# Kernel generation with integer turns and bit-wise fractions, and statistics of eight token tiles moved to ScalarE

## The chip, the cores and the metric

The kernel runs on one core of a Trainium2 chip. The metric is the device time of one execution in microseconds (us), as the median over runs. The engines named below are TensorE (PE; PEld are its weight loads), VectorE (DVE), ScalarE (ACT), GpSimd (POOL) and SyncE (SP, which here only issues transfers). They run side by side; each works through its own instructions in order and waits on semaphores for the others.

## The reference

Four residual layers over x of 2048 tokens and 640 channels: a long convolution (a), attention (b), the same convolution (c), the same attention (d).

```python
def _A_ref(u, A_re, A_im, B_re, B_im, C_re, C_im, log_dt, Dskip):
    dt = jnp.exp(log_dt)[:, None]
    logdA = dt * (A_re + 1j * A_im)
    dB = dt * (B_re + 1j * B_im)
    P = jnp.exp(logdA[:, :, None] * l[None, None, :])        # l = 0..2047
    K = jnp.einsum("dn,dnl,dn->dl", Cc, P, dB).real          # 640 channels, 128 states
    ...                                                      # causal convolution of u with K by FFT
    return y + u * Dskip

x = A_u
x = x + _A_ref(_layernorm(x), ...)
x = x + _B_ref(_layernorm(x), ...)                           # 32 heads, one shared key/value head
x = x + _A_ref(_layernorm(x), ...)
x = x + _B_ref(_layernorm(x), ...)
```

## The kernel before, in words

**Generation of the convolution kernels (`_kgen`, L360).** K[d, l] is a sum over 128 complex exponentials. The position l is split as 32 i + col, so that exp(logdA l) is a product of two factors, each with a size (a real exponential) and an angle. The 640 channels are worked in 20 units of 32 channels. For every unit and each of two halves h (h = 0 the factor over i, h = 1 the factor over col and the phase of C times B):

- `phase_first` (L416): TensorE makes the angles, in turns, as [128, 1024] in PSUM, tile `ph`, which has one buffer.
- `phase` (L424): VectorE takes the whole turns away. `magic_round` (L240, the instruction has L241) adds and subtracts 1.5 * 2^23 into `r` (bf16), then L431 subtracts `r` from `ph` into `f`, a fraction between -1/2 and 1/2; `f` has four buffers.
- `trig` (L433): ScalarE makes `fa` = |f| (L444), sin(2 pi f) (L445) and cos as sin(pi/2 - 2 pi |f|) (L446).
- `sizes` (L449) and `exps` (L457): TensorE makes the exponents in PSUM (`pe`, two buffers, three tiles a unit), ScalarE the exponentials (L462, L464).
- `products` (L466): six VectorE instructions of 128x1024 multiply sizes and sines. `sums` (L483): TensorE sums over the 128 states into `pk`. `store` (L494): ScalarE copies `pk` out, and transfers take it to memory.

The order on TensorE, ScalarE and VectorE is written out by hand in the loop from L519 on: in turn u it works on unit u with `trig`, `sizes` and `exps`, on unit u + 1 with `phase`, on unit u - 1 with `products`, on unit u - 2 with `sums` and on unit u - 3 with `store`. Sine and exponential need different tables on ScalarE; even and odd units therefore order them differently, and one pair of units loads each table once. In turns 5 to 12 VectorE also takes the layer norm's statistics of token tiles 0 to 7 (`stats`, L680: two `bn_stats`, one `bn_aggr`); tiles 8 to 15 follow behind the last unit. In the last turns the weights of the Fourier transform (`wf`, 4 MB) are loaded into the memory that the tables of the generation leave (L578).

**Spectra of the kernels (`kernel_spectra`, L781).** For five chunks of 128 channels, `raw` (L616) makes four products on TensorE, which ScalarE copies out (L631), and `whole` (L645) is a set of butterflies on VectorE (L642, L118, L121) through the common buffer `B`. `raw` of a chunk stands ahead of `whole` of the chunk before it in the order, and takes a hook `ahead(t)` that is called ahead of each of its four products. The spectra are stored to memory and loaded again in the convolution.

**Normalization.** `norm` (L754) turns the statistics `mv` into scale and shift for two groups of token tiles: eight small VectorE instructions and one square root on ScalarE (L747) for each. In `conv_layer` (L802) both calls stand ahead of `kernel_spectra`. The scaled input is first needed by `prepare(0)` (L894, L830) behind the spectra.

The convolution, the attention and layers c and d are not touched.

Of the kernel before, what the change touches and what calls it, by code (L numbers as in the profile page):

```python
# [11 lines left out]
F32 = mybir.dt.float32  # L12
F32R = mybir.dt.float32r
BF16 = mybir.dt.bfloat16
I32 = mybir.dt.int32
AF = mybir.ActivationFunctionType
ALU = mybir.AluOpType
# [4 lines left out]
P = 128  # L22
L = 2048
D = 640
# [4 lines left out]
TWO_PI = 2.0 * math.pi  # L29
# [4 lines left out]
FIRST = (0, 2, 1, 3)  # L34
TAUS = [s + 4 * n for s in FIRST for n in range(4)]
SCALE = 20.0**-0.5
LIMIT = 32.0 * 20.0**0.5
SAFE = ((LIMIT - 1e-6) / 1.002) ** 2
LOG2 = SCALE / math.log(2.0) * 2.0**23
LOWEST = -125.0 * math.log(2.0) / SCALE  # L40
# [149 lines left out]
def weave(calls, between):  # L190

    for i in range(len(calls) + 1):
        for n, call in between:
            if n == i or (i == len(calls) and n > i):
                call()
        if i < len(calls):
            calls[i]()


class Net:  # L200
# [8 lines left out]
    def setup(self, ctx):  # L209
        tc, nc = self.tc, self.nc  # L210
        self.cp = ctx.enter_context(tc.tile_pool(name="cp", bufs=1))
        self.dr = ctx.enter_context(tc.tile_pool(name="dr", bufs=1, space=DRAM))
        self.ident = self.cp.tile([P, P], F32, name="ident")
        self.halfpi = self.cp.tile([P, 1], F32, name="halfpi")
        nc.vector.memset(self.halfpi, 0.5 * math.pi)
        self.xp = ctx.enter_context(tc.tile_pool(name="xp", bufs=1))
        self.x = self.xp.tile([P, 16, D], F32, name="x")
        self.mv = [self.xp.tile([P, 12, 2], F32, name="mv0"), self.xp.tile([P, 4, 2], F32, name="mv1")]
        self.rn = None
        self.placed = {}  # L220
        self.kd = self.dr.tile([NCH, P, 16 * DC], F32, name="kd")
        self.kh = self.dr.tile([NCH, P, 32 * DC], F32, name="kh")
# [137 lines left out]
    def _kgen(self, ctx):  # L360
        tc, nc, ins = self.tc, self.nc, self.ins
        kp = ctx.enter_context(tc.tile_pool(name="kps", bufs=1, space=PSUM))
        early = ctx.enter_context(ExitStack())
# [31 lines left out]
        bp = ctx.enter_context(tc.tile_pool(name="kgb", bufs=2, reuse_waits="tile"))  # L395
# [1 line left out]

        units = [(q, r, q * 256 + 16 * r, 128, 128) for q in range(2) for r in range(8)]
        units += [(2, r, 512 + 16 * r, 64, 64) for r in range(4)]
        C1, S1, C2, S2, M1, M2, E1R, F, PH, PE_, PK, KST = ({} for _ in range(12))  # L400
        KST[0, 0] = bp.tile([P, 64, 32], F32, tag="kst", bufs=2, name="kst00")

        def big(tag, u, x, bufs=2):
# [17 lines left out]
                nc.tensor.matmul(pp[:, 512 * par : 512 * par + 512], grp(src, u, par, rows),  # L421
                                 kg[0:rows, col : col + 512], start=True, stop=True)

        def phase(u, h):  # L424
            if (u, h) not in PH:
                phase_first(u, h)
            pp = PH.pop((u, h))
            r = bp.tile([P, 1024], BF16, tag="r", bufs=2, name=f"r{u}{h}")
            self.magic_round(r, pp)
            F[u, h] = bp.tile([P, 1024], F32, tag="f", bufs=4, name=f"f{u}{h}")  # L430
            nc.vector.tensor_tensor(F[u, h], pp, r, ALU.subtract)  # L431

        def trig(u, h):  # L433
            if h == 0:
                C1[u], S1[u] = big("c1", u, 33), big("s1", u, 33)
                nc.gpsimd.memset(C1[u][:, :, :, 0:1], 1.0)
                nc.gpsimd.memset(S1[u][:, :, :, 0:1], 0.0)
                s, c = swap(S1[u])[:, :, :, 1:33], swap(C1[u])[:, :, :, 1:33]
            else:
                C2[u], S2[u] = big("c2", u, 32, 3), big("s2", u, 32, 3)  # L440
                s, c = swap(S2[u]), swap(C2[u])
            f = F.pop((u, h))
            fa = bp.tile([P, 1024], F32, tag="fa", bufs=1, name=f"fa{u}{h}")
            nc.scalar.activation(fa, f, AF.Abs)  # L444
            nc.scalar.activation(s, f.rearrange("p (a d s) -> p a d s", a=2, d=16), AF.Sin, scale=TWO_PI)  # L445
            nc.scalar.activation(c, fa.rearrange("p (a d s) -> p a d s", a=2, d=16), AF.Sin,  # L446
                                 scale=-TWO_PI, bias=self.halfpi)

# [65 lines left out]
        n = len(units)  # L514
        engines = {mybir.EngineType.PE, mybir.EngineType.Activation, mybir.EngineType.DVE}
        with tc.manual_schedule(engines=engines):
            for h in range(2):
                phase(0, h)
            for u in range(n + 3):  # L519
                now, nxt, prod, tot = u < n, u + 1 < n, 0 < u <= n, 2 <= u < n + 2  # L520
                odd = u % 2 == 1
                if u >= 3:
                    store(u - 3)
                if now and not odd:
                    trig(u, 0)
                if prod:
                    products(u - 1, 0)
                if now:
                    sizes(u, 0)
                    if odd:  # L530
                        exps(u, 0)
                if nxt:
                    phase_first(u + 1, 0)
                if tot:
                    sums(u - 2, range(0, 2))
                if now:
                    sizes(u, 1)
                    if odd:
                        exps(u, 1)
                if tot:  # L540
                    sums(u - 2, range(2, 3))
                if nxt:
                    phase(u + 1, 0)
                if now and odd:
                    sizes(u, 2)
                    exps(u, 2)
                if prod:
                    products(u - 1, 1)
                if now:
                    trig(u, 0 if odd else 1)  # L550
                if tot:
                    sums(u - 2, range(3, 5))
                if nxt:
                    phase(u + 1, 1)
                if prod:
                    products(u - 1, 2)
                if tot:
                    sums(u - 2, range(5, 7))
                if now:
                    if odd:  # L560
                        trig(u, 1)
                    else:
                        exps(u, 0)
                        sizes(u, 2)
                        exps(u, 1)
                        exps(u, 2)
                if tot:
                    sums(u - 2, range(7, 8))
                if u == 0:
                    self.load_x()  # L570
                    nc.sync.dma_start(self.ident, ins["c_id"])
                if 5 <= u < 13:
                    self.stats(u - 5)
                for t in {n: range(8, 12), n + 1: range(12, 16)}.get(u, ()):
                    self.stats(t)
                if u == n:
                    early.close()
                    self.conv_weights(nc.sync)  # L578
# [101 lines left out]
    def stats(self, t):  # L680
# [5 lines left out]
        g, i = self.place(t)  # L686
        nc.vector.bn_aggr(self.mv[g][:, i], st.rearrange("p a b -> p (a b)"))

    def place(self, t):

        return (1, t // 4) if t % 4 == 3 else (0, 3 * (t // 4) + t % 4)
# [86 lines left out]

        self.nc.gpsimd.dma_start(k, self.ins["A_Dskip"][None, c * DC : (c + 1) * DC], accum_op=ALU.add)

    def kernel_spectra(self):  # L781

        nc, cv = self.nc, self.cvp

        ks = [self.scratch("k0").rearrange("p a b -> p (a b)").rearrange("p (t d) -> p t d", t=16)]
        kts = cv.tile([P, 4, 16, DC], F32, tag="wi", name="kts")
        ktl = cv.tile([P, 24, DC], F32, tag="xn", name="ktl")
        self.butterflies()
        ks += [kts[:, c] for c in range(3)] + [ktl[:, 0:16]]
        for c in range(NCH):  # L790
            nc.gpsimd.dma_start(ks[c].rearrange("p t d -> p (t d)"), self.kd[c])
        self.skip(NCH - 1, ks[4][0:1, 0])
        Z = {}
        for c in range(NCH + 1):
            if c < NCH:
                Z[c] = self.raw(ks[c], f"k{c}", c % 4)
            if c > 0:
                A = Z.pop(c - 1)
                weave(self.whole(A, -1, 4 if c == 1 else 1), ())
                nc.sync.dma_start(self.kh[c - 1], A.rearrange("p s d -> p (s d)"))  # L800

    def conv_layer(self, nm, first):  # L802
# [3 lines left out]
        tc, nc, cv = self.tc, self.nc, self.cvp  # L806
# [2 lines left out]
            self.butterflies()  # L809
        with tc.manual_schedule(engines={mybir.EngineType.PE, mybir.EngineType.Activation,  # L810
                                         mybir.EngineType.DVE}):
            if first:
                self.norm(nm, 0)
                self.norm(nm, 1)
            self.norm_next(nm)
            if first:
                self.kernel_spectra()
            else:
                for c in range(2):
                    self.placed[f"{nm}{c}"] = self.spectrum(f"{nm}{c}", c + 1)  # L820
                self.placed["xn"] = self.cvp.tile([P, 24, DC], F32, tag="xn", bufs=1, name=f"xn{nm}0")
# [132 lines left out]
            turn = None  # L954
            for c in range(NCH):
                A = As.pop(c)
# [8 lines left out]
                else:  # L965
# [10 lines left out]
                    if c == NCH - 2:  # L976
                        scr = new_xn("s").rearrange("p a d -> p (a d)")
# [655 lines left out]
```

## Time and profile before

| | |
|---|---|
| median of 3 runs | 2971.92 us (2971.57 to 2973.75) |
| the profiled execution, its time | 2973.82 us |
| its span | 2971.8 us |
| granted TensorE clock, mean | 0.952 |
| PE busy | 2720.8 us, 92% |
| DVE busy | 2375.0 us, 80% |
| ACT busy | 2397.1 us, 81% |
| POOL busy | 293.1 us, 10% |

The span is what the profile covers; 2.0 us of the profiled execution's time lie around it. Busy shares are means over stages that differ: the generation lies between 44 and 300 us of the span, the spectra of the kernels and the first convolution behind it, and the attention, where TensorE is full, takes most of the rest. A row of a timeline holds start, length, engine, line, operation, tile written <- tiles read, shape, count, and in brackets how long the engine stood idle before it and what ended that. A group's row holds the count, the busy time and the mean in ns, and the idle time before its instructions with what ended it.

### The profile page before, as it was taken

The page shows a single profiled execution, that of the slowest core. Times are in us where ns is not written, and L with a number is a line of the kernel's source. Part 1 is how long each engine was busy: PE and PEld are TensorE (multiplying, and loading weights), DVE is VectorE, ACT ScalarE, POOL GpSimd, SP SyncE. Part 2 cuts the span into 40 slices and gives each one's busy share as a digit, 9 for nine tenths or more (in the row PEclk, how much of TensorE's full clock was granted, in tenths as well). Part 3 has the DMA queues.
Part 4 walks back from the last instruction along what each step waited for, and adds up shares of the span by engine and source line. Part 5 has one row for each costly group of instructions (what it writes and reads, how often), then busy time and mean ns, then how long its engine had stood idle before and what let it go on. Part 6 is the DMA issues. An engine that isn't in the chain of part 4 may idle for free. (4 is left out here: it accounts for less than half of the span.)

```text
span 2971.8 us, 71403 instructions
## 1 busy us (share of the span) xinstructions
PE 2720.8 (92%) x29916; PEld 1563.3 (53%) x29916; DVE 2375.0 (80%) x2820; ACT 2397.1 (81%) x3065; POOL 293.1 (10%) x514
## 2 busy tenths in 40 slices
PE   2776989898899999999999999898999999999999
PEld 0333978775344444444444688773444444444444
DVE  7999899943678888888888699826788888878885
ACT  5888243444899999999999734337999999999997
POOL 0000001100201011010101011001111110101101
PEclk9655999998999999999999999898999999999999
DMA  6113555533211111111111255231111211211211
GB/s 146 35 17 99 172 183 114 119 122 104 84 36 33 35 33 36 35 35 37 31 36 34 92 114 126 87 127 54 34 34 35 55 33 37 51 35 33 54 32 31
DMA packets 156101, 196.30 MB, mean 66 GB/s; under 512 B 66221, under 2 KB 123533, under 8 KB 152149
## 3 DMA queue, kind: packets, MB, share of 16 engines
q1 hardware_dynamic: 119704, 141.90, 16.2%
q0 software_dynamic: 33776, 48.08, 8.0%
q8 instruction: 239, 3.92, 0.5%
q10 hardware_dynamic: 2288, 1.64, 0.2%
q14 instruction: 94, 0.76, 0.1%
HBM read 111.47 MB, written 48.55 MB: 54 GB/s over the span
## 5 line engine op out<-in xcount | busy, mean ns | idle before, releaser
L1346 ACT ACTIVATE pw<-pw 128x1024 f32<-128x1024 f32 (+3 forms) x840 | 765.6, 957 | 0.0
L1323 ACT ACTIVATE pt<-scb 128x1024 f32<-128x1024 f32 x684 | 699.3, 1133 | 23.2 <-PE scb L1313 21.5
L1323 ACT ACTIVATE pt<-scd 128x1024 f32<-128x1024 f32 x684 | 703.8, 1148 | 11.7 <-PE scd L1313 5.6
L1338 DVE COPY pw<-scd 128x1024 f32<-128x1024 f32 x307 | 375.2, 1222 | 81.6 <-PE scd L1313 65.5
L1338 DVE COPY pw<-scb 128x1024 f32<-128x1024 f32 x307 | 374.7, 1221 | 79.8 <-PE scb L1313 64.1
L1313 PE MATMUL scb<-qpb,kt 62*128 62x512 f32 x2048 | 367.4, 446 | 29.3 <-DVE pw L1338 13.6
L1313 PE MATMUL scd<-qpd,kt 62*128 62x512 f32 x2048 | 366.5, 445 | 19.8 <-ACT pt L1323 7.5
L1377 PE MATMUL pob<-pt,vt 128*32 128x256 f32 x5472 | 368.1, 387 | 0.0
L1377 PE MATMUL pod<-pt,vt 128*32 128x256 f32 x5472 | 367.6, 386 | 0.0
L1313 PEld LDWEIGHTS scb<-qpb,kt 62*128 62x128 f32 x2048 | 169.8, 186 | 252.8 <-ACT pt L1323 146.8
L1313 PEld LDWEIGHTS scd<-qpd,kt 62*128 62x128 f32 x2048 | 169.0, 186 | 245.0 <-ACT pt L1323 154.6
L1363 DVE SCALAR_TENSOR_TENSOR zh<-zh,zm 128x1024 f32<-128x1024 f32 x198 | 239.7, 1210 | 0.0
L1377 PEld LDWEIGHTS pob<-pt,vt 128*32 128x32 f32 x5472 | 143.3, 109 | 166.8 <-issue 108.0
L1377 PEld LDWEIGHTS pod<-pt,vt 128*32 128x32 f32 x5472 | 143.3, 109 | 164.6 <-issue 105.8
L1377 PE MATMUL pob<-pw,vt 128*32 128x256 f32 x2456 | 164.8, 381 | 0.4 <-ACT pw L1346 0.4
L1377 PE MATMUL pod<-pw,vt 128*32 128x256 f32 x2456 | 163.9, 379 | 0.4 <-ACT pw L1346 0.4
L1409 POOL DMA_DIRECT2D dn<-on x62 | 43.6, 703 | 1192.7 <-DVE on L1408 1155.6
L1415 POOL DMA_DIRECT2D rc<-ivd x248 | 125.8, 513 | 115.4 <-DMA ivd<-dn 111.6
L1446 DVE TENSOR_TENSOR x<-pyd,x 128x320 f32<-128x320 f32 x147 | 71.7, 488 | 77.9 <-PE pyd L1459 77.8
L1446 DVE TENSOR_TENSOR x<-pyb,x 128x320 f32<-128x320 f32 x147 | 71.7, 488 | 77.1 <-PE pyb L1459 77.0
L1459 PE MATMUL pyb<-wo,ot 128*32 128x320 f32 x1176 | 106.7, 434 | 5.3 <-DVE on L1408 4.5
L1459 PE MATMUL pyd<-wo,ot 128*32 128x320 f32 x1176 | 106.7, 434 | 4.4 <-DVE on L1408 3.6
(391 smaller groups left out, 4139.8 us busy)
## 6 DMA issues: line engine op xcount, KB each, us to landing
Akh<-kh SPq DMA_DIRECT2D x10, 2048.0 KB
rc<-ivd POOLq DMA_DIRECT2D x248, 64.0 KB, 2.2
kh<-Ak SPq DMA_DIRECT2D x5, 2048.0 KB
qhd<-qh SPq DMA_DIRECT2D x40, 256.0 KB
qld<-ql SPq DMA_DIRECT2D x40, 256.0 KB
qpb<-qhd SPq DMA_DIRECT2D x256, 40.0 KB
qpd<-qhd SPq DMA_DIRECT2D x256, 40.0 KB
ot<-on SPq DMA_DIRECT2D x216, 40.0 KB
```

The source lines that it names most:

```text
L1313: nc.tensor.matmul(sc[:, 512 * par : 512 * par + 512], kt[rows, 128 * t : 128 * t + 128], qps[nb, hg][rows, f].rearrange("p a c -> p (a c) ...
L1323: nc.scalar.activation(pt, sc, AF.Exp, scale=SCALE)
L1338: nc.vector.tensor_copy(cols, sc)
L1346: nc.scalar.activation(cols, cols, AF.Exp, scale=SCALE)
L1363: nc.vector.scalar_tensor_tensor(h, a, c[k], f, op0=ALU.add, op1=ALU.mult)
L1377: nc.tensor.matmul(po[32 * j : 32 * j + 32, 256 * f : 256 * f + 256], v[:, t], pt[j], start=(t == 0), stop=(t == 15))
L1409: nc.gpsimd.dma_start(den, on[20:128:32].rearrange("j (c r) -> j c r", c=32))
L1415: nc.gpsimd.dma_start(inv[32 * j : 32 * j + 32], self.ivd[hg % 2, j : j + 1].to_broadcast([32, 512]))
L1446: nc.vector.tensor_tensor(xh, py, xh, ALU.add)
L1459: nc.tensor.matmul(py[j : j + m], o[:, 128 * i + j : 128 * i + j + m], w[:, c0 : c0 + n], start=start, stop=stop)
```

## The change

In `_kgen` the angle is turned into an integer in units of 2^-23 turns (plus half a turn), straight from PSUM; an and-mask keeps the fraction, and an or sets the exponent bits, so that the result, read as float, is 1 + fraction. ScalarE's `Abs` and first `Sin` take the offset back out as a bias, a [128, 1] column (`middle`, `turn`). The rounded tile `r` is replaced by `z` (one buffer).

The statistics of token tiles 0 to 7 leave the loop. `stats_scalar` takes each on ScalarE: a copy with the sum, the mean, a square with the sum, with a part of the buffer `B` as scratch. Four stand ahead of the first `raw`, three in its hook, one behind it. `stats_done` scales them into `mv` on VectorE, and the two `norm` calls move from `conv_layer` to behind `whole` of the first chunk.

```diff
+EARLY = (0, 1, 2, 4, 5, 6, 3, 7)
...
+        self.turn = self.cp.tile([P, 1], F32, name="turn")
+        nc.vector.memset(self.turn, -3.0 * math.pi)
+        self.middle = self.cp.tile([P, 1], F32, name="middle")
+        nc.vector.memset(self.middle, -1.5)
...
-        def phase(u, h):
+        def turns(u, h):
             if (u, h) not in PH:
                 phase_first(u, h)
             pp = PH.pop((u, h))
-            r = bp.tile([P, 1024], BF16, tag="r", bufs=2, name=f"r{u}{h}")
-            self.magic_round(r, pp)
-            F[u, h] = bp.tile([P, 1024], F32, tag="f", bufs=4, name=f"f{u}{h}")
-            nc.vector.tensor_tensor(F[u, h], pp, r, ALU.subtract)
+            Z[u, h] = bp.tile([P, 1024], I32, tag="z", bufs=1, name=f"z{u}{h}")
+            nc.vector.tensor_scalar(Z[u, h], pp, 2.0**23, 2.0**22, ALU.mult, ALU.add)
+
+        def fraction(u, h):
+            f = bp.tile([P, 1024], I32, tag="f", bufs=4, name=f"f{u}{h}")
+            nc.vector.tensor_scalar(f, Z.pop((u, h)), 0x7FFFFF, 0x3F800000, ALU.bitwise_and, ALU.bitwise_or)
+            F[u, h] = f.bitcast(F32)
+
+        def phase(u, h):
+            turns(u, h)
+            fraction(u, h)
...
-            nc.scalar.activation(fa, f, AF.Abs)
-            nc.scalar.activation(s, f.rearrange("p (a d s) -> p a d s", a=2, d=16), AF.Sin, scale=TWO_PI)
+            nc.scalar.activation(fa, f, AF.Abs, bias=self.middle)
+            nc.scalar.activation(s, f.rearrange("p (a d s) -> p a d s", a=2, d=16), AF.Sin, scale=TWO_PI,
+                                 bias=self.turn)
...
-                if 5 <= u < 13:
-                    self.stats(u - 5)
...
+    def stats_scalar(self, k):
+        nc, early = self.nc, self.early
+        A, t = nc.scalar.activation, EARLY[k]
+        scr = self.B[:, 0:8].rearrange("p s d -> p (s d)")[:, 1024 * (k % 2) : 1024 * (k % 2) + D]
+        A(scr, self.x[:, t], AF.Copy, accum_out=early["sum"][:, k : k + 1])
+        A(early["shift"][:, k : k + 1], early["sum"][:, k : k + 1], AF.Copy, scale=-1.0 / D)
+        A(scr, self.x[:, t], AF.Square, bias=early["shift"][:, k : k + 1], accum_out=early["sq"][:, k : k + 1])
+
+    def stats_done(self):
+        for g, a, b in ((0, 0, 6), (1, 6, 8)):
+            for i, (n, f) in enumerate((("shift", -1.0), ("sq", 1.0 / D))):
+                self.nc.vector.tensor_scalar(self.mv[g][:, 0 : b - a, i], self.early[n][:, a:b], f, None, ALU.mult)
...
-    def kernel_spectra(self):
+    def kernel_spectra(self, nm):
...
+        for k in range(4):
+            self.stats_scalar(k)
+
+        def ahead(t):
+            if t > 0:
+                self.stats_scalar(3 + t)
+
         for c in range(NCH + 1):
             if c < NCH:
-                Z[c] = self.raw(ks[c], f"k{c}", c % 4)
+                Z[c] = self.raw(ks[c], f"k{c}", c % 4, ahead=ahead if c == 0 else lambda t: None)
+            if c == 0:
+                self.stats_scalar(7)
             if c > 0:
                 A = Z.pop(c - 1)
                 weave(self.whole(A, -1, 4 if c == 1 else 1), ())
+                if c == 1:
+                    self.stats_done()
+                    self.norm(nm, 0)
+                    self.norm(nm, 1)
                 nc.sync.dma_start(self.kh[c - 1], A.rearrange("p s d -> p (s d)"))
...
             if first:
-                self.norm(nm, 0)
-                self.norm(nm, 1)
...
-                self.kernel_spectra()
+                self.kernel_spectra(nm)
```

More of the change, by code (lines that the diff above doesn't have):

```diff
@@ L399, in _kgen @@
         units += [(2, r, 512 + 16 * r, 64, 64) for r in range(4)]
-        C1, S1, C2, S2, M1, M2, E1R, F, PH, PE_, PK, KST = ({} for _ in range(12))
+        C1, S1, C2, S2, M1, M2, E1R, F, FA, Z, PH, PE_, PK, KST = ({} for _ in range(14))
         KST[0, 0] = bp.tile([P, 64, 32], F32, tag="kst", bufs=2, name="kst00")
@@ L792, in kernel_spectra @@
         self.skip(NCH - 1, ks[4][0:1, 0])
+        self.early = {n: self.xp.tile([P, 8], F32, tag=f"ea{n}", bufs=1, name=f"ea{n}") for n in ("sum", "shift", "sq")}
+        for k in range(4):
[3 more added lines that the diff above has]
+                self.stats_scalar(3 + t)
         Z = {}
@@ L811, in conv_layer @@
                                          mybir.EngineType.DVE}):
-            if first:
-                self.norm(nm, 0)
-                self.norm(nm, 1)
             self.norm_next(nm)
             if first:
-                self.kernel_spectra()
+                self.kernel_spectra(nm)
             else:
```

## The prediction

> **What bounds the kernel now.** I read the table of stretches first, to see which engine is full in the generation of the kernels (the loop over 20 units, 44 to 300 us) and behind it, then the groups by line, then the timelines of ScalarE, TensorE and VectorE over one loop turn. In a row of the table stand busy time and instructions of PE, PEld, DVE, ACT and POOL, the granted clock, the DMA share and GB/s.
>
> ```profile
> 200.00:240.00 40.00, 31.47 (x468) 14.09 (x468) 39.62 (x37) 33.77 (x35) 1.86 (x8) 0.50 0.20 28
> 340.00:360.00 20.00, 20.00 (x182) 20.00 (x181) 19.69 (x26) 5.44 (x6) 0.00 (x0) 1.00 0.25 106
> ```
>
> VectorE looks like the bound of the generation (39.62 of 40), and ScalarE looks idle for 6 us of 40. The groups of the first 560 us say what ScalarE waits for.
>
> ```profile
> L431 DVE TENSOR_TENSOR f<-ph,r 128x1024 f32<-128x1024 f32 x40 | 49.0, 1225 | 2.0
> L241 DVE TENSOR_SCALAR r<-ph 128x1024 bf16<-128x1024 f32 x40 | 48.7, 1218 | 7.7 <-PE ph L421 7.4 <-DMA hdare<-hare 0.3
> ...
> L446 ACT ACTIVATE c<-fa,halfpi 128x1024 f32<-128x1024 f32 x40 | 45.7, 1142 | 0.0
> ...
> L445 ACT ACTIVATE s<-f 128x1024 f32<-128x1024 f32 x40 | 42.2, 1056 | 0.1
> L444 ACT ACTIVATE fa<-f 128x1024 f32<-128x1024 f32 x40 | 42.1, 1052 | 6.0 <-DVE f L431 5.3
> L462 ACT ACTIVATE m<-pe 128x1024 f32<-128x1024 f32 x40 | 39.8, 1022 | 18.8 <-PE pe L454 18.4
> ...
> L685 DVE BATCH_NORM_STATS2 st<-x 128x6 f32<-128x320 f32 x32 | 13.8, 472 | 0.0
> ...
> L707 ACT ACTIVATE xnas<-x,smshifta 128x384 f32<-128x384 f32 x4 | 2.4, 605 | 0.0
> ...
> L703 ACT ACTIVATE xnas<-x 128x384 f32<-128x384 f32 x4 | 2.0, 508 | 0.0
> ```
>
> ScalarE waits for the fractions `f` of VectorE 5.3 us in 40 times, nearly all of it before the first, and 18.4 us for `pe`, the exponents that TensorE makes. So it is a loop of ScalarE and TensorE that has its own period. ScalarE, one turn of two units, with first and last turn:
>
> ```profile
> 65.06 1.05 ACT L444 ACTIVATE fa<-f 128x1024 f32<-128x1024 f32 x1
> ...
> 184.55 1.02 ACT L462 ACTIVATE m<-pe 128x1024 f32<-128x1024 f32 x1 [2.25 <-PE pe L454]
> ...
> 209.86 1.02 ACT L462 ACTIVATE m<-pe 128x1024 f32<-128x1024 f32 x1 [2.74 <-PE pe L454]
> ...
> 234.23 1.02 ACT L462 ACTIVATE m<-pe 128x1024 f32<-128x1024 f32 x1 [1.80 <-PE pe L454]
> 235.78 1.02 ACT L464 ACTIVATE m<-pe 128x1024 f32<-128x1024 f32 x1 [0.53 <-PE pe L454]
> 236.70 1.05 ACT L444 ACTIVATE fa<-f 128x1024 f32<-128x1024 f32 x1
> ...
> 261.06 1.05 ACT L444 ACTIVATE fa<-f 128x1024 f32<-128x1024 f32 x1
> ...
> 284.58 1.05 ACT L444 ACTIVATE fa<-f 128x1024 f32<-128x1024 f32 x1
> ```
>
> Nine turns from 65.06 to 284.58 take 24.39 each. VectorE, with no statistics left, needs less for the same turn, 255.39 - 232.14 = 23.25:
>
> ```profile
> 232.14 1.22 DVE L472 TENSOR_TENSOR e1r<-m,c 128x1024 f32<-128x1024 f32 x1
> ...
> 255.39 1.22 DVE L472 TENSOR_TENSOR e1r<-m,c 128x1024 f32<-128x1024 f32 x1
> ```
>
> Yet ScalarE takes 24.36 from 236.70 to 261.06, so the lead that VectorE gains is of no use to it. Its waits of 1.80 and 0.53 come from TensorE's own queue:
>
> ```profile
> 228.81 1.01 PE L454 MATMUL pe<-kg,tm 96*128 96x512 bf16 x2 [1.47 <-ACT m L462]
> ...
> 233.16 1.03 PE L454 MATMUL pe<-kg,tm 48*128 48x512 bf16 x2
> ```
>
> TensorE starts when ScalarE's exponential has freed a `pe` slot (1.47 <-ACT) and then works without a gap through the order of the program until 233.16 + 1.03, when the exponential at 234.23 can start. No VectorE instruction ends a wait in it, so the chain is as long with a faster VectorE. Behind the generation, from 333 us on, VectorE is the bound (19.69 of 20).
>
> **The change, part by part.** *VectorE in the generation.* The rounding from PSUM stays one instruction from PSUM (1218 ns); the subtraction (1225 ns, L431) becomes an integer and/or from SBUF to SBUF, of which the attention has one of this size:
>
> ```profile
> L1359 DVE TENSOR_SCALAR zm<-z 128x1024 int32<-128x1024 int32 x24 | 16.5, 689 | 0.6
> ```
>
> 40 x (1225 - 689) = 21.4 us less, and 16 of the 32 statistics instructions go, 16 x 0.472 = 7.6 us. I cost this 29 us at nothing, because the loop of ScalarE and TensorE covers it, except for two things. First, where VectorE lagged: the waits at 184.55 and 209.86 are 0.45 and 0.94 above the 1.80 of the other turns: -1.4 us. Second, the start, where `ph` has one buffer and TensorE waits for the subtraction to release it:
>
> ```profile
> 55.04 1.23 DVE L241 TENSOR_SCALAR r<-ph 128x1024 bf16<-128x1024 f32 x1 [5.03 <-PE ph L421]
> 56.30 1.22 DVE L431 TENSOR_TENSOR f<-ph,r 128x1024 f32<-128x1024 f32 x1
> ...
> 57.67 1.01 PE L421 MATMUL ph<-kg,ta 96*128 96x512 bf16 x2 [1.81 <-DVE f L431]
> 58.47 2.03 PE L454 MATMUL pe<-kg,tm 96*128 96x512 bf16 x4
> ...
> 59.57 1.02 ACT L464 ACTIVATE m<-pe 128x1024 f32<-128x1024 f32 x1 [2.33 <-PE pe L454]
> ...
> 63.18 1.02 ACT L462 ACTIVATE m<-pe 128x1024 f32<-128x1024 f32 x1 [1.62 <-PE pe L454]
> ```
>
> `ph` becomes free at 55.04 + 1.23 instead of 56.30 + 1.22, so the matmul at 57.67 and the exponential at 59.57 come 1.25 sooner; the same release comes once more ahead of 63.18 (0.76 of it), together -2.0 us.
>
> *ScalarE in the generation.* Abs (L444) and the first Sin (L445) get a bias from a [128,1] tile. The second Sin has one already: 1142 ns against 1052 and 1056, same size. Square with such a bias against Copy (L707, L703): 605 against 508. So 0.09 us each, on the engine that sets the period; from the Abs at 65.06 to the last group of exponentials lie units 1 to 18, 36 halves of two instructions: 72 x 0.09 = +6.5 us. Bounds: 0 (hidden in the pipeline) and 72 x 0.097 = 7.0; I take 0.09, because ScalarE has no wait in that part of the turn which could hide it. Sum at the end of the loop: -2.0 - 1.4 + 6.5 = +3.1 us.
>
> *Between loop and spectra.* The weight load and the first products wait for the loop's end, so they move by 3.1.
>
> ```profile
> 283.65 5.16 SPq L607 DMA_DIRECT2D wf<-in_c_wf  x8
> 300.22 1.28 ACT L747 ACT_TABLE_LOAD   x1
> ...
> 307.12 1.03 ACT L631 ACTIVATE Ak<-zk 128x1024 f32<-128x1024 f32 x1 [1.19 <-PE zk L629]
> ...
> 332.14 1.03 ACT L631 ACTIVATE Ak<-zk 128x1024 f32<-128x1024 f32 x1 [2.55 <-PE zk L629]
> ```
>
> The four tiles of statistics that now stand ahead of the copies: from L703 and L707 with 256 elements more at 0.84 ns (the 1052 against 508 ns over 640 elements), 0.72 + 0.82, with the small shift and accumulator reads some 1.9 each, 7.5 us from 303.5 (300.22 + 3.1, and 0.2 of the last unit's own biases) on: done at 311.0, against 307.12 + 3.1 = 310.2 for the first copy. That is 0.8 late once; TensorE's pace, (332.14 - 307.12) / 7 = 3.57 us per copy, leaves room for the other four beside copies of 1.03: nothing on the path. Two columns set at the start lie beside the loading of the inputs. No transfer is moved past another on SP's or POOL's queue; the first spectrum's store, issued behind the normalizations now, waits for its butterflies alone.
>
> *The two normalizations.* They were in VectorE's idle time ahead of 307; they come between the first and second kernel's butterflies, where VectorE is the bound.
>
> ```profile
> 304.16 0.23 DVE L748 RECIPROCAL rs0a<-sq0a 128x12 f32<-128x12 f32 x1
> ...
> 307.17 0.17 DVE L769 TENSOR_SCALAR nmrm1a<-nmr1a 128x4 f32<-128x4 f32 x1
> ...
> 328.89 2.50 DVE L121 SCALAR_TENSOR_TENSOR Ak<-B 128x512 f32<-128x512 f32 x4
> 333.19 2.29 DVE L642 TENSOR_TENSOR B<-Ak 128x2048 f32<-128x2048 f32 x1 [1.80 <-ACT Ak L631]
> ```
>
> VectorE ends the first kernel at 331.39 and waits 1.80 for the copy at 332.14. The root of the first normalization is on ScalarE, queued behind that copy, and needs a table load (1.28 at 300.22) behind it: 333.17 + 3.1 + 1.3 + 0.2 = 337.8. The four scalings of the new sums lie in that wait. Then reciprocal to last scaling, 304.16 to 307.34: 3.2. So the second kernel starts at 341.0 instead of 333.19: +7.8. Queued behind: four more kernels' butterflies and the convolution on VectorE, which has hardly a wait to give it back (the largest to 540 us):
>
> ```profile
> DVE B L642 <- issue: 1.9, 1, 1.9
> ```
>
> Bounds of this step: +1.3 beyond the shift (3.2 less the 1.80 wait, if the root comes early) and +4.7. I take the upper, since the queue's order fixes it. **Sum: +7.8 us.** The profiled execution has a span of 2971.8 in a time of 2973.82; by the sum 2979.6 and 2981.6. The median of the three runs, 2971.92, lies 1.9 below it, so I forecast 2979.7 for the median.
>
> **A rule weighed.** All matmuls of the turn shown have the slow duration (1.03 for two), and the clock of its stretch is 0.50, although TensorE works there without a gap from 228.81 to past 233.16 + 1.03, 5.4 us. The Trainium skill, "TensorE: Matmul & The Clock Gate", Part 1, says that some 3.4 us of sustained work release the full clock. This trace disagrees here. By the rows the sum stays at +7.8; by the rule, with nothing of VectorE interrupting TensorE, it would be the second rival's, -13.2.
>
> **The rivals.** *The bias is hidden.* For it: instructions of ScalarE overlap (235.78 + 1.02 is past 236.70). Against it: the second Sin's extra is whole in its duration. Then the loop ends 3.4 us sooner, the copy at 329.8, the root at 331.2, the second kernel at 334.4: +1.2, 2973.1.
>
> *The waits for `pe` shrink (faster).* If TensorE, freed of VectorE's releases, ran the chain at 228.81 at full clock, its 5.4 us would be some 2.7 and the waits of 1.80 and 0.53 would go: 9 x 2.33 = 21.0 us, 7.8 - 21.0 = -13.2 in all, 2958.7. It decides from 1.5 us per turn on (13.7 in all: 7.8 and the 5.9 of 0.2%). For it: VectorE's full row, and TensorE's waits for `f` (1.81 at 57.67). Against it: the turn at 236.70, where VectorE leads, has the same waits; a longer lead only lengthens TensorE's idle time ahead of the chain.
>
> *The scratch waits.* The statistics write into the butterflies' buffer, from 303.5 on. If its memory is free only when the last kernels' stores have gone out,
>
> ```profile
> 300.23 13.00 SPq L508 DMA_DIRECT2D kd<-kst  x8
> ```
>
> then at 313.2 + 3.3 = 316.5: four tiles until 324.0, then four copies and three tiles (4 x 1.03 + 3 x 1.9) until 333.8 instead of 318.9, the first kernel's end 15 later at 346.3, and 0.5 + 4.1 for scalings and normalizations: the second kernel at 351, +17.8, 2989.7. Against it: the loop's products end before the stores are out, and only a memory that the store itself reads would wait.
>
> That the integer step is no shorter than the subtraction changes nothing: VectorE would still need 23.3 per turn against 25.1.
>
> **How the numbers follow.** The forecast 0.58 (own range 2977 to 2983: the bounds of the bias, and the normalizations at +3 to +5); hidden bias or a partly given-back normalization, 2970 to 2977, 0.19; shrinking waits 0.14; scratch 0.09. 0.2% is 5.9 us, about what a measurement of this kernel can tell from no change. Some of the forecast's lower edge is inside it: slower 0.62, same 0.23, faster 0.15. The range 2968 to 2985 leaves out the shrinking waits and the scratch's upper part.
>
> **What would show it.** Right: L444 and L445 at some 1.14 us, 25.1 us from one Abs of an odd unit to the next, the same 1.80 ahead of the exponential; VectorE's busy share in the generation below nine tenths with waits for ScalarE; the weight load issued at 286.8; the root behind a table load at about 337 and the second kernel's butterflies at 341. Wrong: turns of 23 us or less, matmuls of 0.6 in the exponents' chain, or the copy of the first product long after 311.

## The result, and the profile after

The changed kernel takes 2979.52 us (median of 11 runs, 2978.28 to 2980.43), the kernel before 2972.37 us (11 runs beside them, 2971.57 to 2973.77): a ratio of 1.0023, 95% interval 1.0015 to 1.0031. The prediction said 2979.7. The profiled execution took 2979.44 us with a span of 2977.6, 5.8 more than the 2971.8 before.

VectorE first. The stretch of the generation that the prediction showed, and the groups of the first 560 us of the changed kernel (count, busy us, mean ns, idle us ahead of them and what ended that):

```profile
200.00:240.00 40.00, 25.52 (x392) 11.39 (x395) 32.15 (x32) 34.71 (x35) 2.06 (x8) 0.54 0.21 28
```
```profile
L459 ACT ACTIVATE s<-f,turn 128x1024 f32<-128x1024 f32 x40 | 46.0, 1149 | 0.1
L458 ACT ACTIVATE fa<-f,middle 128x1024 f32<-128x1024 f32 x40 | 45.8, 1144 | 5.4 <-DVE f L440 4.8
...
L477 ACT ACTIVATE m<-pe 128x1024 f32<-128x1024 f32 x40 | 40.0, 1023 | 16.8 <-PE pe L469 16.3
L440 DVE TENSOR_SCALAR f<-z 128x1024 int32<-128x1024 int32 x40 | 27.8, 696 | 2.0
L487 DVE TENSOR_TENSOR e1r<-m,c 128x1024 f32<-128x1024 f32 x20 | 24.4, 1221 | 27.1 <-PE pk L506 23.8 <-ACT c L461 3.4
```

VectorE is no longer full: 32.15 of 40 us against 39.62. The fraction costs 696 ns where the subtraction cost 1225, as intended. VectorE now idles 27.1 us ahead of its products, where it waits for others, and the turn did not get shorter for it. ScalarE still waits for `pe` (16.3 us ahead of L477; 18.4 before), and its Abs and first Sin are 1144 and 1149 ns instead of 1052 and 1056. ScalarE over one turn of two units, with the first and the last Abs of an odd unit:

```profile
63.42 1.14 ACT L458 ACTIVATE fa<-f,middle 128x1024 f32<-128x1024 f32 x1
...
213.78 1.14 ACT L458 ACTIVATE fa<-f,middle 128x1024 f32<-128x1024 f32 x1
...
236.41 1.03 ACT L477 ACTIVATE m<-pe 128x1024 f32<-128x1024 f32 x1 [1.80 <-PE pe L469]
237.96 1.02 ACT L479 ACTIVATE m<-pe 128x1024 f32<-128x1024 f32 x1 [0.52 <-PE pe L469]
238.88 1.14 ACT L458 ACTIVATE fa<-f,middle 128x1024 f32<-128x1024 f32 x1
...
288.24 1.14 ACT L458 ACTIVATE fa<-f,middle 128x1024 f32<-128x1024 f32 x1
```

A turn takes 25.10 us (213.78 to 238.88), against 24.36, with the same waits of 1.80 and 0.5. On TensorE the chain is as long as before (the exponential follows 5.42 us behind its start, 236.41 - 230.99 and 234.23 - 228.81); what has grown is the idle time ahead of it, from 1.47 to 6.49:

```profile
230.99 1.01 PE L469 MATMUL pe<-kg,tm 96*128 96x512 bf16 x2 [6.49 <-ACT m L477]
```

Behind the loop: the weight load on SP's queue, ScalarE's first statistics, first and last copy of products, the root, and VectorE from the root to the second kernel's butterflies:

```profile
287.32 4.58 SPq L620 DMA_DIRECT2D wf<-in_c_wf  x8
```
```profile
303.95 0.73 ACT L707 ACTIVATE B<-x 128x640 f32<-128x640 f32 x1
...
311.58 1.00 ACT L644 ACTIVATE Ak<-zk 128x1024 f32<-128x1024 f32 x1
...
333.65 1.02 ACT L644 ACTIVATE Ak<-zk 128x1024 f32<-128x1024 f32 x1 [2.55 <-PE zk L642]
334.69 1.28 ACT L775 ACT_TABLE_LOAD   x1
```
```profile
336.23 0.23 DVE L776 RECIPROCAL rs0a<-sq0a 128x12 f32<-128x12 f32 x1 [2.32 <-ACT sq0a L775]
...
339.32 2.28 DVE L655 TENSOR_TENSOR B<-Ak 128x2048 f32<-128x2048 f32 x1
```

The second kernel's butterflies start at 339.32 instead of 333.19: +6.1 us, and the span ends 5.8 later.

### The profile page after: what moved, and what is told of

Its sections match the earlier page's. It is cut to its first block, busy times and chain, and to the rows that moved or that the text cites. A ratio compares the mean times of both kernels' runs of the same rounds, so it can differ in the third digit from the quotient of the medians.

```text
span 2977.6 us, 71455 instructions
## 1 busy us (share of the span) xinstructions
PE 2717.0 (91%) x29916; PEld 1565.0 (53%) x29916; DVE 2347.8 (79%) x2802; ACT 2419.5 (81%) x3105; POOL 294.9 (10%) x514
## 3 DMA queue, kind: packets, MB, share of 16 engines
q10 hardware_dynamic: 2288, 1.64, 0.2%
## 5 line engine op out<-in xcount | busy, mean ns | idle before, releaser
L1362 ACT ACTIVATE pt<-scb 128x1024 f32<-128x1024 f32 x684 | 700.2, 1135 | 23.4 <-PE scb L1352 16.7
L1352 PE MATMUL scd<-qpd,kt 62*128 62x512 f32 x2048 | 367.7, 445 | 18.4 <-ACT pt L1362 7.9
L469 PE MATMUL pe<-kg,tm 48*128 48x512 bf16 (+1 forms) x120 | 58.9, 592 | 63.7 <-ACT m L477 56.1
```

The lines of the kernel that those rows point to most:

```text
L469: nc.tensor.matmul(pe[:, 512 * h : 512 * h + 512], grp(tm, u, par, rows), kg[0:rows, col : col + 512], start=True, stop=True)
L1352: nc.tensor.matmul(sc[:, 512 * par : 512 * par + 512], kt[rows, 128 * t : 128 * t + 128], qps[nb, hg][rows, f].rearrange("p a c -> p (a c) ...
L1362: nc.scalar.activation(pt, sc, AF.Exp, scale=SCALE)
```

## The experiments

The theory: in the generation ScalarE and TensorE's queue set the turn; a bias is paid whole, a faster VectorE is not seen, and the moved normalizations cost what they hold up. In the first four runs one thing is done at a time (the kernel before beside them: 2972.0 us); in the next three TensorE's part of the turn is changed (2973.3); the last has 2971.32 beside it.

**The bias alone.** The kernel before, with a [128, 1] column of zeros as bias:

```diff
-            nc.scalar.activation(fa, f, AF.Abs)
+            nc.scalar.activation(fa, f, AF.Abs, bias=self.zero)
-            nc.scalar.activation(s, ..., AF.Sin, scale=TWO_PI)
+            nc.scalar.activation(s, ..., AF.Sin, scale=TWO_PI, bias=self.zero)
```

> The kernel before, with a [128,1] column of zeros as the bias of Abs and of the first Sin; nothing else is changed. If ScalarE's loop with TensorE sets the period, and the column costs 0.09 us each, a turn grows from 24.37 to 25.1 us, the two lags of VectorE (1.4 us) vanish in it, the weight load is issued some 5 us later than at 283.65, and the time is 2977 to 2979 against 2972. If VectorE sets the period (39.6 of 40 busy), the longer instructions fill ScalarE's idle time and the time stays within 2 us. If the bias is hidden in the pipeline, the two groups stay at 1.05 us and nothing moves.

Measured: 2980.54 us (2978.93 to 2981.56), ratio 1.0026 [1.0015, 1.0037]. The group of Abs, the weight load and the second kernel's start:

```profile
L446 ACT ACTIVATE fa<-f,zero 128x1024 f32<-128x1024 f32 x40 | 45.8, 1144 | 6.0 <-DVE f L433 5.3
```
```profile
289.12 4.87 SPq L610 DMA_DIRECT2D wf<-in_c_wf  x8
```
```profile
336.94 2.29 DVE L645 TENSOR_TENSOR B<-Ak 128x2048 f32<-128x2048 f32 x1 [1.81 <-ACT Ak L634]
```

Adding zero costs 92 ns on each Abs, the weight load comes 5.5 us later, and the time is lost with no other part of the change in it; at 8.5 us the loss lies above the 5 to 7 that were expected. That the bias might be hidden is disproved.

**The integers alone.** The changed kernel with statistics and normalizations back where they were:

```diff
+                if 5 <= u < 13:
+                    self.stats(u - 5)
...
-        for k in range(4):
-            self.stats_scalar(k)
...
-                if c == 1:
-                    self.stats_done()
-                    self.norm(nm, 0)
-                    self.norm(nm, 1)
...
+            if first:
+                self.norm(nm, 0)
+                self.norm(nm, 1)
```

> The change's integer generation alone: statistics in the loop and both normalizations ahead of the spectra, as before. If ScalarE and TensorE set the period, the loop is that of the changed kernel, 25.1 us a turn, because VectorE with 21.3 and the statistics is still below it; the weight load comes 3.7 us later than before, the second kernel's butterflies 1.5 to 3.7 us later, and the time is 2973.5 to 2976. If VectorE sets the period, 21 us of it are saved in the loop and the time is 2950 to 2955.

Measured: 2973.65 us (2972.19 to 2975.22), ratio 1.0006 [0.9997, 1.0015].

```profile
200.00:240.00 40.00, 27.16 (x412) 12.33 (x408) 34.20 (x36) 34.70 (x36) 2.05 (x8) 0.54 0.22 28
```
```profile
287.25 4.39 SPq L622 DMA_DIRECT2D wf<-in_c_wf  x8
```
```profile
333.97 2.29 DVE L657 TENSOR_TENSOR B<-Ak 128x2048 f32<-128x2048 f32 x1 [1.81 <-ACT Ak L646]
```

The turn is 25.1 us, though VectorE has 5.8 of 40 us to spare, and the loop ends as late as with the whole change (287.25 against 287.32). The second kernel starts 0.78 later than before (1.5 to 3.7 were expected), so the 3.6 of the loop's end are mostly made up between the two; how is told below.

**Statistics and normalizations alone.** The kernel before with the second half of the change (the functions `stats_scalar` and `stats_done`, and the moved `norm` calls as in the diff of the change), and with the rounding and subtraction in floats as before.

> The change's other part alone: float rounding and no bias in the generation, statistics of eight tiles on ScalarE behind it, normalizations between the first and second kernel. If ScalarE and TensorE set the period, turns stay at 24.4 us, only the lags of 1.4 us go, the normalizations and their root cost 4.6 us on VectorE from the second kernel on, and the time is 2974 to 2976. If VectorE sets the period, its 8.3 us of statistics come off the loop and the time is 2968 or less.

Measured: 2975.43 us (2973.97 to 2977.19), ratio 1.0010 [1.0001, 1.0019].

```profile
282.08 4.47 SPq L610 DMA_DIRECT2D wf<-in_c_wf  x8
```
```profile
328.29 1.02 ACT L634 ACTIVATE Ak<-zk 128x1024 f32<-128x1024 f32 x1 [2.55 <-PE zk L632]
```
```profile
333.96 2.29 DVE L645 TENSOR_TENSOR B<-Ak 128x2048 f32<-128x2048 f32 x1
```

Turns are 24.37 from the second to the eighth and the loop ends 1.6 us earlier, the lag of VectorE that the prediction found and hardly more. Then the root, queued behind the copy, holds VectorE. From the last copy to the second kernel's start lie 333.96 - 328.29 = 5.67 us, with the whole change 339.32 - 333.65 = 5.67, before 333.19 - 332.14 = 1.05: the moved normalizations cost 4.62.

**TensorE's order, on the kernel before.** In odd units the three sizes, each followed by its exponential, go ahead of the next unit's phase and of the group sums on TensorE:

```diff
                 if now:
                     sizes(u, 0)
                     if odd:
                         exps(u, 0)
+                        for k in (1, 2):
+                            sizes(u, k)
+                            exps(u, k)
...
-                if now:
+                if now and not odd:
                     sizes(u, 1)
-                    if odd:
-                        exps(u, 1)
...
-                if now and odd:
-                    sizes(u, 2)
-                    exps(u, 2)
```

> The kernel before with another order on TensorE alone: in odd units the three groups of exponents stand together, ahead of the next unit's angles and of the sums. If the waits of 1.80 and 0.53 us come from TensorE's queue, they fall to about 0.2, ScalarE's own turn is then 22.2 us, and VectorE with 23.3 a turn and 8.3 us of statistics becomes the bound: it had only 3.5 us of waits in the loop, so the time falls by 1 to 4 us, to 2968 to 2971. If the waits come from the slow clock alone, or from VectorE, they stay and so does the time.

Measured: 2969.37 us (2968.0 to 2972.07), ratio 0.9992 [0.9983, 1.0001].

```profile
L462 ACT ACTIVATE m<-pe 128x1024 f32<-128x1024 f32 x40 | 38.9, 1021 | 0.6
L464 ACT ACTIVATE m<-pe 128x1024 f32<-128x1024 f32 x20 | 20.5, 1023 | 23.5 <-PE pe L454 18.9 <-DVE s L481 4.5
```
```profile
233.23 1.05 ACT L444 ACTIVATE fa<-f 128x1024 f32<-128x1024 f32 x1
...
256.48 1.05 ACT L444 ACTIVATE fa<-f 128x1024 f32<-128x1024 f32 x1
```
```profile
200.00:240.00 40.00, 30.60 (x468) 14.20 (x468) 39.62 (x37) 33.91 (x36) 1.87 (x8) 0.50 0.20 28
```

The waits of 1.80 are gone (L462: 0.6 us in all 40), but 23.5 us stand ahead of L464. Most of them are put down to `pe`, whose matmuls stand in TensorE's queue behind those of `ph`, and these wait for VectorE's `f` (1.40 us at 248.53). A turn without statistics takes 23.25, which is VectorE's own time for it (255.39 - 232.14 in the prediction), and VectorE has no room left (39.62 of 40). With the queue's chain out of the way VectorE is the bound at once. The two sit only 1.1 us per turn apart. The gain of 2.6 us is hardly clear of the noise: the interval touches 1.

**The same order on the changed kernel.**

> The changed kernel, with TensorE's order in odd units altered as in the run of that order on the kernel before (the three sizes of an odd unit, each followed by its exponential, ahead of the next unit's phase and the group sums); arithmetic, statistics and normalizations are the changed kernel's. Theory (ScalarE and TensorE's queue set the turn): the waits of 1.80 and 0.53 us ahead of the exponentials go, and VectorE, at 32 of 40 us, does not step in as it did on the kernel before: a turn of 25.1 - 2.2 = 22.9 us, some 20 us less in nine turns, the weight load's issue at about 267 instead of 287, the time at about 2960 (2957 to 2965). Rival (ScalarE's own work is the whole period, and its waits are only taken up elsewhere): turns stay at 24.5 or above, time 2974 or more. Rival (VectorE's statistics and round-downs are what the change was about): the order gives no more here than the 2.6 us that it gave on the kernel before, so about 2977.

Measured: 2958.1 us (2955.84 to 2959.5), ratio 0.9951 [0.9938, 0.9965].

```profile
L477 ACT ACTIVATE m<-pe 128x1024 f32<-128x1024 f32 x40 | 38.9, 1021 | 0.6
L479 ACT ACTIVATE m<-pe 128x1024 f32<-128x1024 f32 x20 | 20.5, 1023 | 4.2 <-PE pe L469 4.2
```
```profile
206.96 1.14 ACT L458 ACTIVATE fa<-f,middle 128x1024 f32<-128x1024 f32 x1
...
252.46 1.14 ACT L458 ACTIVATE fa<-f,middle 128x1024 f32<-128x1024 f32 x1
```
```profile
200.00:240.00 40.00, 26.64 (x500) 13.68 (x492) 38.20 (x37) 39.36 (x39) 1.89 (x8) 0.67 0.21 28
```

Two turns take 45.50, one 22.75, and ScalarE is full (39.36 of 40). The same edit gave 2.6 us on the kernel before and gives 21.4 on the changed one (2979.52 to 2958.1): VectorE's freed time was real, and TensorE's order was what kept it from being used. This is the direct test of the theory.

**Keeping TensorE busy instead.** The changed kernel in its own order; in even units one group's sums are made 16 times more in the idle 6.5 us, and write the results that were there before:

```diff
                         exps(u, 0)
+                        if tot:
+                            for _ in range(16):
+                                sums(u - 2, range(7, 8))
                         sizes(u, 2)
```

> The changed kernel, with one group's sums (that of the unit two before) made 16 times instead of once in even units, ahead of the third size's matmuls, in the 6.5 us in which TensorE waits for the magnitude there; the repeats write what was written before. It asks whether the chain of matmuls behind that wait is slow because TensorE was idle just before it. Theory A (a chain warms only after some 9 to 10 us without a gap, as the traces of both kernels show): the clock comes up in the middle of the chain, the waits of 1.80 and 0.53 shrink in part, turns of 23.5 to 24.5, time 2968 to 2976. Theory B (3.4 us of sustained work are enough): the chain runs at full speed from its start, all of the 2.3 us per turn go, time about 2959. Theory C (the clock does not answer to such filling): turns of 25.1 or somewhat more, since the repeats may run into the chain's start, time 2979 to 2985.

Measured: 2967.98 us (2963.47 to 2971.8), ratio 0.9984 [0.9975, 0.9993]. The profile is of the fastest run. TensorE and the table of stretches in one turn:

```profile
228.87 0.44 PE L506 MATMUL pk<-e1r,c 128*32 128x64 f32 x8 [0.86 <-DVE c L495]
230.00 0.44 PE L506 MATMUL pk<-m,s 128*32 128x64 f32 x8 [0.69 <-DVE s L496]
...
236.42 0.28 PE L506 MATMUL pk<-e1r,c 128*32 128x64 f32 x8
```
```profile
230.00:236.00 6.00, 5.86 (x140) 3.88 (x144) 5.97 (x6) 5.97 (x8) 0.17 (x1) 0.50 0.01 3
236.00:242.00 6.00, 5.27 (x257) 4.20 (x250) 4.99 (x6) 5.97 (x6) 0.16 (x1) 0.97 0.02 5
```
```profile
238.08 1.28 ACT L477 ACT_TABLE_LOAD   x1
239.38 1.94 ACT L477 ACTIVATE m<-pe 128x1024 f32<-128x1024 f32 x2
...
260.23 1.28 ACT L477 ACT_TABLE_LOAD   x1
```

The filling takes the clock to full some 7 us after 228.87, in time for the chain. In this turn the exponentials no longer wait, and from one table load to the next it takes 22.15 us instead of 25.1. So the waits were indeed made of slow matmuls, and there are two ways out: another order, or a fast clock. The size fell between two of the expectations. In the profiled run the turns are as Theory B had them (22.80 in the mean, from 77.80 to 260.23 in eight), but the clock comes up only after some 7 us of work and not after 3.4, and the runs spread over 8 us, where the changed kernel spreads over 2. In the last turn of that run the waits are back (2.32 us ahead of the exponential at 268.28, a turn of 25.38). That more turns miss the clock in the slower runs is my reading and not shown; only the fastest was profiled.

**Order, and a fraction without a bias.** TensorE's order as above, statistics and normalizations as before, and the fraction made a signed 32-bit integer by one shift, which ScalarE reads as it is:

```diff
-            nc.vector.tensor_scalar(Z[u, h], pp, 2.0**23, 2.0**22, ALU.mult, ALU.add)
+            nc.vector.tensor_scalar(Z[u, h], pp, 2.0**23, None, ALU.mult)
...
-            nc.vector.tensor_scalar(f, Z.pop((u, h)), 0x7FFFFF, 0x3F800000, ALU.bitwise_and, ALU.bitwise_or)
-            F[u, h] = f.bitcast(F32)
+            nc.vector.tensor_scalar(f, Z.pop((u, h)), 9, None, ALU.logical_shift_left)
+            F[u, h] = f
...
-            nc.scalar.activation(fa, f, AF.Abs, bias=self.middle)
+            nc.scalar.activation(fa, f, AF.Abs)
-            nc.scalar.activation(s, ..., AF.Sin, scale=TWO_PI, bias=self.turn)
+            nc.scalar.activation(s, ..., AF.Sin, scale=TWO_PI / 2.0**32)
...
-                                 scale=-TWO_PI, bias=self.halfpi)
+                                 scale=-TWO_PI / 2.0**32, bias=self.halfpi)
```

> The same TensorE order; the generation is by integers, but the fraction is taken with one left shift by 9 bits into a signed 32-bit integer, which ScalarE reads as it is with 2 pi / 2^32 as its scale, so that neither Abs nor the first Sin has a bias column; statistics and normalizations are as in the kernel before. Theory: no bias takes 0.74 us from each turn of the run with the order alone: 22.2 us per turn in those without statistics, 23.4 (VectorE's 21.3 and 2.1) in the four with statistics; nine turns are some 18 us shorter than the 219.5 of the kernel before, the weight load's issue at about 264, the second kernel's start some 18 us before the 333.19 of the kernel before, time 2950 to 2956. Rival (an integer input costs ScalarE as much as the bias column did, 0.1 us per instruction): turns of 22.9, time about 2958 to 2962. Rival (a biasless turn is bound by TensorE's slow chain instead): turns of 23.2 as in the order's run on the kernel before, time about 2965.

Measured: 2948.73 us (2946.33 to 2950.32), ratio 0.9918 [0.9904, 0.9931], the fastest of all.

```profile
L459 ACT ACTIVATE s<-f 128x1024 f32<-128x1024 int32 x40 | 42.2, 1056 | 0.1
L458 ACT ACTIVATE fa<-f 128x1024 f32<-128x1024 int32 x40 | 42.1, 1052 | 5.4 <-DVE f L440 4.8
```
```profile
261.39 4.87 SPq L620 DMA_DIRECT2D wf<-in_c_wf  x8
```
```profile
307.78 2.29 DVE L655 TENSOR_TENSOR B<-Ak 128x2048 f32<-128x2048 f32 x1 [1.80 <-ACT Ak L644]
```

An integer input costs ScalarE nothing (1052 and 1056 ns, as with floats). Turns take 21.7 to 22.2 us behind the first, two of those with statistics 23.0 and 23.5 (four turns of some 23.4 were expected). The weight load is 22.3 us earlier than before, at 261.4 where about 264 was expected; the second kernel starts 25.4 earlier, where some 18 was expected, and the time lies below the expected 2950 to 2956.

**The second half of the change on top.** The same, with the statistics on ScalarE and the moved normalizations (the diff of the change) put back:

> The run with the signed fraction and TensorE's new order, with the second half of the change put back: the statistics of eight tiles by ScalarE behind the generation, and the normalizations with them. It asks what that half is worth where VectorE and not TensorE's queue is ScalarE's next partner: there four turns with statistics take some 23.2 us against 22.1 in the others (tiles' waits for VectorE's s). Theory: those four turns fall to 22.1 as well, 4 to 5 us earlier at the weight load; behind it the statistics and the square roots give back 2.3 us (the statistics alone on the kernel before: weight load 1.57 us earlier, second kernel 0.77 us later) to 5.4 us (the changed kernel against the integers alone at the second kernel: 339.32 against 333.97): the time 2946 to 2951, no difference that can be told. Rival (with ScalarE as the bound everywhere, the whole 7.6 us of statistics and the 4.6 us of the square roots are exposed): weight load 4.5 earlier, the second kernel 8 later, time 2955 or more. Rival (the statistics on VectorE held the whole loop up): turns fall in all of the loop, time below 2944.

Measured: 2949.86 us (2949.6 to 2954.36), ratio 0.9931 [0.9917, 0.9944].

```profile
259.03 5.69 SPq L618 DMA_DIRECT2D wf<-in_c_wf  x8
```
```profile
304.35 1.02 ACT L642 ACTIVATE Ak<-zk 128x1024 f32<-128x1024 f32 x1 [2.55 <-PE zk L640]
```
```profile
310.01 2.28 DVE L653 TENSOR_TENSOR B<-Ak 128x2048 f32<-128x2048 f32 x1
```

All turns behind the first fall to 22.1 us or less and the weight load comes 2.4 us earlier (4 to 5 were expected, from four longer turns; only two had been longer). From the last copy to the second kernel lie 310.01 - 304.35 = 5.66 us again, 4.6 more than without, and the start is 2.2 later. The time can't be told from the run without this half. So it gains up to what VectorE held up and pays the 4.6 of the normalizations in every version.

## Why the prediction was right, point by point

- *VectorE's 29 us at nothing:* shown for the turn: the group of fractions fell by 21 us, and the turn is 25.10 with it and without. Not nothing in the time: the integers alone (with the same bias) are 6.9 us faster than the bias alone. 1.9 of that is there at the weight load, from the start's release of `ph` (the Abs at 63.42 against 65.28); 3.0 at the second kernel; the rest belongs to what stays open.
- *The lag, -1.4:* shown. Nine turns take 288.24 - 63.42 = 224.82; the 219.52 of before, plus 9 x 0.74 of bias, less 1.39 of lag make 224.79. Taking only the statistics out of the loop brings its end 1.57 forward.
- *The start, -2.0:* measured -1.64 (65.06 to 63.42). The first of the two `ph` matmuls comes only 0.71 sooner (56.96 instead of 57.67, where 1.25 was expected), because TensorE's first `pe` waited 0.64 longer for a transfer of the tables (53.78 instead of 53.14).
- *The bias, +6.5:* measured 6.66 (nine turns), and shown on its own by the bias of zeros (nine turns 5.24 longer, in which the 1.39 of lag vanish too). The Trainium skill, "ScalarE: Activation LUTs", section "What ACT_TABLE_LOAD costs", gives 93 ns for each [128, 1] operand; the 92 ns of the groups agree.
- *The loop's end, +3.1:* measured +3.67.
- *The products move by 3.1:* **the term that was mis-sized.** The last copy went from 332.14 to 333.65, +1.5. The first products started 3.6 later, but ran faster:

```profile
302.63 15.18 PE L629 MATMUL zk<-Rk,wf 128*128 128x128 f32 x119 [1.89 <-issue]
```
```profile
306.21 13.11 PE L642 MATMUL zk<-Rk,wf 128*128 128x128 f32 x116 [1.29 <-issue]
```
```profile
304.00:308.00 4.00, 4.00 (x28) 4.00 (x27) 2.62 (x18) 1.21 (x3) 0.00 (x0) 0.71 0.82 208
```
```profile
304.00:308.00 4.00, 2.71 (x26) 2.63 (x25) 3.76 (x12) 3.87 (x12) 0.00 (x0) 1.00 0.97 381
```

  First before, then after, in both pairs: the granted clock between 304 and 308 is 0.71 before and 1.00 after, so 2.1 of the 3.6 us come back, an estimated 1.7 of them by the clock (119 products at the later pace would take 13.45) and the rest because 12 products instead of 9 had run ahead of this wait. I had moved the work without asking which clock it would meet there; why the clock fell in one case and not in the other is not shown. The integers alone meet the same full clock. The zero bias, whose last sums and first products fall between 304 and 308, has 0.67 there and the full clock only from 308 on; it goes from 1.9 us behind the integers alone at the weight load to 3.0 at the second kernel.
- *Statistics beside the products:* shown. They are done at 311.58 (I had 311.0), and from the fifth copy on TensorE's pace (2.55 of waiting each) has absorbed them. (The 0.84 ns per element in the working is 0.85 by its own two durations, which changes nothing.) The rival of the scratch is disproved: they start at 303.95, as soon as ScalarE is free.
- *The normalizations, +4.7:* measured 4.62, 4.62 and 4.61. (The lower bound of +1.3 should read +1.4, which is 3.2 less 1.80.)
- *The sum, +7.8:* the second kernel came at +6.13. The median is 7.15 higher, the span 5.8.
- *The rule weighed:* by it the waits would have gone. They stayed, and the clock with them: 0.54 in the stretch shown. The rival had the right size for its own mechanism: with a full clock the turn falls to some 22.8, but it needs work in the idle time, not a lighter VectorE alone.

**What stays open.** Against the kernel before, the span's end follows the second kernel's start only within -1.9 to +2.9 us (the changed kernel -0.3, the zero bias +2.9, the statistics alone +1.9, the new order on the changed kernel -1.9). Part of it can be placed in the first convolution. Up to the butterflies that start at 475.21 before, every run keeps its second kernel's shift within 0.3 us; at those that start at 554.20 before, the changed kernel has lost 1.4 us more, the integers alone 2.2, the statistics alone 2.8 and the zero bias nothing. The rest arises behind them and was not settled. These are differences of single executions, and the kernel before alone ran between 2970.27 and 2975.76 in the 29 runs beside the first four experiments. The near agreement of 2979.7 with 2979.52 is therefore in part luck: the second kernel came 1.7 us sooner than the sum had it, but the median rose by 1.0 more than the second kernel's shift, and the kernel before came out 0.45 higher (2972.37, where the forecast started from 2971.92).

## What to carry to other kernels

A full engine need not be the bound: look for whose wait ends last in the stage, and try the order of that engine's queue before making the full one faster. When two limits lie within a few per cent, either change alone gives next to nothing (the integers +1.7 us, the order -2.6, neither clear of the noise) and both together give the gain (-15.2 with the statistics and normalizations moved as well; -21.5 with these and without the bias; -24.6 without either). Count what a cheaper operation hands to the next engine: a bias column of 0.09 us, 72 times on ScalarE's path, cost 8.5 us when it was added alone, and the 21 us saved on VectorE brought back 6.9.

## What the runs showed of the hardware that was not expected

- Small work in TensorE's idle time changes its clock for what follows: 0.50 to 0.97 in the stretches above, some 7 us after TensorE had become nearly gapless (9 us in the next turn, 251.00 to 260.2). The Trainium skill, "TensorE: Matmul & The Clock Gate", Part 1, has 3.4 us of sustained work for it; this turn needed about twice that. In the changed kernel itself TensorE works without a gap from 230.99 and is still slow ten us later:

```profile
230.00:241.00 11.00, 10.01 (x152) 4.59 (x155) 7.51 (x7) 8.43 (x9) 0.31 (x2) 0.50 0.31 43
```

  Behind the loop of the same run it took only some 4 us: TensorE starts on the last sums at 298.92, and the clock is 0.50 from 300 to 302, 0.67 from 302 to 304 and 1.00 from 304 to 308. What decides between 4 and 10 us is not shown; the work differs (sums alone behind the loop, exponents, phases and sums mixed in the chain).

```profile
298.92 0.44 PE L506 MATMUL pk<-e1r,c 128*32 128x64 f32 x8 [7.33 <-DVE c L495]
```

- ScalarE reads a 32-bit integer input at the speed of a float one: 1052 and 1056 ns for 128x1024 in both.
- Each of ScalarE's sums over a row is an instruction of its own behind the operation, 0.19 us, which is part of the 1.9 us per tile.
